# Block 0's last pair of heads placed by TensorE with 0/1 matrices instead of transfers, with one transfer per weight pair and an order of work that counts transfers

## The chip, the cores and the metric

The kernel runs on one core of one Trainium2 chip. The metric is device time in microseconds (us) of one execution; lower is better. Each kernel was run several times, in rounds that alternate with the kernel before on the same chip. An execution more than 1.5% above the fastest of its kernel counts as slow and is left out; only one in this study was (one run of the kernel before at 1269.63 us, about twice its usual time). A ratio is the mean time of one kernel's fast runs over that of the other kernel's fast runs of the same rounds, so it is not quite the ratio of the medians that are quoted beside it.

TensorE multiplies matrices, VectorE and ScalarE work on elements, GpSimd does some element work beside VectorE, and SyncE issues transfers (DMA). In the traces they are PE, DVE, ACT, POOL and SP; PEld is TensorE's loading of weights. "L466" is line 466 of the kernel's own file, so the same instruction has another number in another kernel: the up products are L466 before and L520 after.

## The reference

A linear attention with a decaying state feeds a dense layer with a gate. Cut to what matters:

```python
def _attn_ref(r, k, v, w, u):            # (4, 8, 768, 48) each; u is (8, 48)
    for t in range(S):
        cur = einsum('bhd,bhe->bhde', u[None] * kt, vt)
        y[:, :, t] = einsum('bhd,bhde->bhe', rt, state + cur)
        state = wt[:, :, :, None] * state + einsum('bhd,bhe->bhde', kt, vt)

def _moe_ref(x, w_in, w_out):            # (3072, 384), (384, 2048), (2048, 384); both weights reach the kernel as float64
    h = x @ w_in
    g = h * np.clip(h + 3.0, 0.0, 6.0) / 6.0
    return (g @ w_out).astype(np.float32)

x = attn_out.transpose(0, 2, 1, 3).reshape(B * S, H * D)     # 384 columns: 8 heads of 48
```

## The kernel before: the parts that matter here

The 768 steps of a sequence are cut into chunks of 128; there are 24 chunks in all, and three of them make a **block** of 384 rows of x. For each chunk the attention is turned into products (scans of the decay on VectorE, a score product, a masked copy, a "read"). For each block there follow 16 **ups** (x times a slice of w_in), each with a ramp on ScalarE and a gate on VectorE, and 48 **downs** (times a slice of w_out, for one chunk each). The weights arrive as float64 and are made into float32 once, pair by pair, by five passes: two on ScalarE, three on VectorE (a shift, a join and an add).

A small scheduler in the kernel (`Plan`) takes every step with an engine, an estimated duration and a priority, and emits the instructions of each engine in the order it finds. Until the first up, it fills TensorE's gaps with products of the identity ("filler"), which nobody reads; they only keep TensorE busy.

The eight heads form four pairs of 2 x 48 rows, and xT wants 3 times 128 rows: three pairs fill rows 0–47 and 64–111 of each third, and the *last pair* is cut into six pieces of 16 rows that go to the rows left free. Before the change small transfers do this, from tile x3 (named "x" in the trace) to xT:

```python
def leave(i):                                   # ScalarE: read's result out of PSUM
    ...
    for g in range(2):
        rows = slice(g * GP, g * GP + D)
        nc.scalar.copy(out=b["xT"][rows, :, now], in_=y_ps[rows, 0:3 * NCC - 2:3, :])
        nc.scalar.copy(out=b["x3"][rows, now], in_=y3[rows, :])

def last_pair(bk, c0, c1, g, q):                # three transfers of 16 rows each
    b = blocks[bk]
    cols, to = slice(c0 * L, c1 * L), g * GP + D
    for j in range(NCC):
        q.dma_start(out=b["xT"][to:to + X3, j, cols], in_=b["x3"][g * GP + j * X3:g * GP + (j + 1) * X3, cols])
...
            if c == BC - 1 or i == SPLIT - 1:   # in block 0 once for chunks 0 and 1, once for chunk 2
                c0 = 0 if i == SPLIT - 1 or bk > 0 else SPLIT
                for g in range(2):
                    q = nc.scalar if i < BC and g == 1 else nc.sync
                    plan.add(f"move{i}.{g}", "ACT" if i < BC and g else "SP", 1.8, do(last_pair, bk, c0, c + 1, g, q), ...)
```

A pair of weight slices is fetched by two transfers of 384 KB, and the priorities of the first chunks, of the weight conversions and of the ups of block 0 are constants tuned by hand:

```python
BEHIND = (-1, -1, 0, 4, 8, 10)
SPLIT = 2
START = (-52.0, -47.1, -26.0, 6.5, 11.0, 9.2)
CONV = (-45.0, 3.1)
UP = (-35.0, 1.4, -31.8, 2.0)
...
            for x in range(2):
                nc.sync.dma_start(out=to[:, x * m:(x + 1) * m], in_=srcs[x])
```

Of the kernel before, what the change touches and what calls it, by code (L numbers as in the profile page):

```python
# [8 lines left out]
F32 = mybir.dt.float32  # L9
# [9 lines left out]
L = 128  # L19
# [6 lines left out]
BEHIND = (-1, -1, 0, 4, 8, 10)  # L26
EARLY = 3
SPLIT = 2
START = (-52.0, -47.1, -26.0, 6.5, 11.0, 9.2)
CONV = (-45.0, 3.1)  # L30
UP = (-35.0, 1.4, -31.8, 2.0)
# [43 lines left out]
class Plan:  # L75
# [10 lines left out]

    def __init__(self):
        self.steps = {}
        self.rings = {}
# [4 lines left out]
    def add(self, name, engine, us, emit, after=(), key=0.0, hold=(), port=False, kb=0.0, lands=0.0):  # L94

        assert name not in self.steps, name
        self.steps[name] = (engine, us, emit, tuple(after), key, tuple(hold), port, kb, lands)

    def order(self):
        steps = self.steps  # L100
        start, end = {}, {}
        free, held = {}, {r: [] for r in self.rings}
        link = port = 0.0
        left = {n: sum(a not in end for a in x[3]) for n, x in steps.items()}
        users = {}
        for n, x in steps.items():
            for a in x[3]:
                assert a in steps, (n, a)
                users.setdefault(a, []).append(n)
        open_ = {n for n, k in left.items() if k == 0}  # L110
        out = []
        while open_:
            best = {}
            for n in open_:
                engine, us, _, after, key, hold, shared, _, _ = steps[n]
                t = free.get(engine, 0.0)
                for a in after:
                    if steps[a][0] != engine:
                        t = max(t, end[a] + self.HOP)
                for r, _ in hold:  # L120
                    over = len(held[r]) - self.rings[r]
                    if over >= 0:
                        ends = sorted(max(end[a] + (self.HOP if steps[a][0] != engine else 0.0) for a in frees)
                                      for frees in held[r] if all(a in end for a in frees))
                        if len(ends) <= over:
                            t = None
                            break
                        t = max(t, ends[over])
                if t is None:
                    continue  # L130
                if shared:
                    t = max(t, port)
                best.setdefault(engine, []).append((t, key, n))
            assert best, sorted(open_)
            t, engine = min((min(c)[0], e) for e, c in best.items())
            _, _, n = min((key, t_, n) for t_, key, n in best[engine] if t_ <= t + 1e-9)
            _, us, _, _, _, hold, shared, kb, lands = steps[n]
            start[n] = t
            free[engine] = end[n] = t + us
            if kb:  # L140

                done = max(link, end[n]) + kb / self.RATE if kb > 32 else end[n]
                link = max(link, done) if kb > 32 else link
                end[n] = max(done + self.LAND, lands)
            if shared:
                port = t + us
            for r, frees in hold:
                held[r].append(frees)
            out.append(n)
            open_.remove(n)  # L150
            for u in users.get(n, ()):
                left[u] -= 1
                if left[u] == 0:
                    open_.add(u)
        assert len(out) == len(steps), [n for n in steps if n not in end]
        self.start, self.end = start, end
        return out
# [15 lines left out]
def fast_path(tc, feat, tok, wflat, ub, moe_w_in, moe_w_out, out, flag, n_chunks):  # L173
# [18 lines left out]
    with ExitStack() as ctx:  # L192
# [20 lines left out]
        w_in = const.tile([128, NFC, NCC, 128], F32, name="w_in")  # L213
        w_out = const.tile([128, NFC, DM], F32, name="w_out")

        def constants():
# [12 lines left out]
            nc.gpsimd.tensor_copy(out=mask, in_=mask_f)  # L229

# [29 lines left out]
        def fetch(j):  # L260
            which, f = pairs[j]
            if which == "in":
                srcs = [moe_w_in[:, (f + x) * 128:(f + x + 1) * 128].rearrange("(c p) j -> p c j", p=128)
                        for x in range(2)]
                dst = w_in[:, f:f + 2].rearrange("p f c j -> p (f c) j")
            else:
                srcs = [moe_w_out[(f + x) * 128:(f + x + 1) * 128, :].rearrange("p (c j) -> p c j", j=128)
                        for x in range(2)]
                dst = w_out[:, f:f + 2].rearrange("p f (c j) -> p (f c) j", j=128)
            m = dst.shape[1] // 2  # L270
            if f64:
                bits = io.tile([128, 2 * m * 128], I64, name="bits", bufs=3)
                to = bits.rearrange("p (c j) -> p c j", j=128)
                conv[j].update(lo=bits.bitcast(U32).rearrange("p (j two) -> p j two", two=2)[:, :, 0],
                               hi=bits.bitcast(I32).rearrange("p (j two) -> p j two", two=2)[:, :, 1],
                               dst=dst.rearrange("p c j -> p (c j)").bitcast(I32))
            else:
                to = dst
            for x in range(2):
                nc.sync.dma_start(out=to[:, x * m:(x + 1) * m], in_=srcs[x])  # L280
# [22 lines left out]
        def high_low(j):  # L303
            c = conv[j]
            nc.vector.tensor_tensor(out=c["dst"], in0=c["top"], in1=c["more"].bitcast(I32), op=ALU.add)  # L305
# [102 lines left out]
        def read(i):  # L408
            d = st[i]
            first = i % n_chunks == 0  # L410
            y_ps = d["y_ps"] = pp.tile([128, 2, P, L], F32, name="two", bufs=2)
            started = set()

            def into(p, g):
                bank, at = PLACES[p]
                rows = (g ^ bank) * GP
                fresh = (bank, rows) not in started
                started.add((bank, rows))
                return dict(out=y_ps[rows:rows + D, bank, at, :], start=fresh, skip_group_check=True)

            if not first:
                for x in range(2):
                    for p in (x, 2 + x):
                        for g in range(2):
                            rows = slice(g * GP, g * GP + D)
                            nc.tensor.matmul(lhsT=d["S"][rows, p, :], rhs=d["R"][rows, p, :], stop=False, **into(p, g))  # L426
# [8 lines left out]
            for p in range(P):  # L435
                for g in range(2):
                    nc.tensor.matmul(lhsT=d["v"][:, 2 * p + g, :], rhs=d["A"][:, 2 * p + g, :],  # L437
                                     stop=(p == 1 or p == P - 1), **into(p, g))
# [22 lines left out]
        def up(bk, f, c0, c1):  # L461
# [3 lines left out]
            for j in range(NCC):  # L465
                nc.tensor.matmul(h_ps[:, :m], lhsT=w_in[:, f, j, :], rhs=b["xT"][:, j, cols],  # L466
# [95 lines left out]
        PB = NFC + BC * 4  # L562

# [5 lines left out]
        for i in range(NT):  # L569
# [37 lines left out]
            if not first:  # L607
                plan.add(f"decay{i}", "DVE" if dve else "POOL", 0.35 if dve else 0.5, do(decay, i),
                         [f"state{i - 1}", f"back{i}"], t - 0.1 if i < len(START) else t - 5, [("S", [f"read{i}"] + [f"state{i}"] * turn)], port=True)
            plan.add(f"read{i}", "PE", 1.0 + 0.55 * turn + 0.6 * (not first), do(read, i),  # L610
                     [f"above{i}"] + [f"turned{i}"] * turn + [f"decay{i}"] * (not first)
                     + [f"up{j}.{NFC - 1}" + "." * (j == 0) for j in (i // BC - 2,) if j >= 0],
                     t + 0.01, [("two", [f"leave{i}"])] + [("ps", [f"state{i}"])] * turn)
            bk, c = divmod(i, BC)
            plan.add(f"leave{i}", "ACT", 1.46, do(leave, i), [f"read{i}"], t + 0.5,
                     [("x", [f"up{bk}.{f}" for f in range(NFC)] + [f"up{bk}.{f}." for f in range(NFC)] * (bk == 0))]
                     if c == 0 else ())
            if c == BC - 1 or i == SPLIT - 1:
                c0 = 0 if i == SPLIT - 1 or bk > 0 else SPLIT
                for g in range(2):  # L620
                    q = nc.scalar if i < BC and g == 1 else nc.sync
                    plan.add(f"move{i}.{g}", "ACT" if i < BC and g else "SP", 1.8, do(last_pair, bk, c0, c + 1, g, q),
                             [f"leave{j}" for j in range(bk * BC + c0, i + 1)], k - 20, kb=1)
# [3 lines left out]
        for j in range(len(pairs)):  # L627
            t = CONV[0] + j * CONV[1]
            plan.add(f"fetch{j}", "SP", 0.9, do(fetch, j), key=t - 20, kb=768 if f64 else 384,
# [9 lines left out]
        for bk in range(NB):  # L639
            subs = [(0, SPLIT, ""), (SPLIT, BC, ".")] if bk == 0 else [(0, BC, "")]  # L640
            last_up = [f"up{bk - 1}.{NFC - 1}" + "." * (bk == 1)] if bk else []
            for c0, c1, x in subs:
                m = c1 - c0
                for f in range(NFC):
                    k = PB * bk + f if bk else UP[0] + f * UP[1] if c0 == 0 else UP[2] + f * UP[3]
                    w = f"{ready}{f // 2}"
                    name = f"{bk}.{f}{x}"
                    i = bk * BC + c1 - 1
                    plan.add(f"up{name}", "PE", 0.645 * m, do(up, bk, f, c0, c1),
                             [w] + last_up + [f"up{bk}.{f}"] * (x == ".") + [f"leave{j}" for j in range(bk * BC + c0, bk * BC + c1)]  # L650
                             + [f"move{i}.{g}" for g in range(2)], k, [("mm", [f"gate{name}"])])
# [4 lines left out]
                             [f"ramp{name}"] + [f"gate{bk}.{f}"] * (x == "."), k - 3,  # L656
                             [("g", downs)] if c0 == 0 else ())
            for c in range(BC):
                for q in range(NFC // 2):
                    k = PB * bk + NFC + c * 4 + q / 2  # L660
                    x = "." if bk == 0 and c >= SPLIT else ""
# [360 lines left out]
```

## Time and profile before

| Kernel before | |
|---|---|
| time, median of 3 runs (range) | 630.24 us (628.9 to 631.51) |
| the execution that was profiled | 626.47 us, span in the trace 624.7 us |
| TensorE busy | 604.4 us, 97% of the span |
| first up product begins | 37.27 us |
| first up product of block 1 begins | 127.01 us |

I cut the span at the two moments of the table. The view of windows of the kernel before gives for each stretch: its length, then busy time (and instructions) of PE, PEld, DVE, ACT and POOL, then TensorE's granted clock as a share of full speed, the share of the DMA engines that was busy, and GB/s.

```profile
0.00:37.27 37.27, 25.46 (x260) 23.62 (x261) 28.30 (x40) 18.47 (x39) 9.17 (x15) 0.94 0.95 279
37.27:127.01 89.74, 86.67 (x609) 63.78 (x609) 72.15 (x107) 54.06 (x137) 33.90 (x27) 0.97 0.61 189
127.01:619.30 492.29, 492.25 (x2394) 300.83 (x2394) 170.69 (x249) 143.02 (x356) 81.41 (x74) 1.00 0.26 81
```

In the last 492 us TensorE alone sets the time: it is busy throughout, at full clock. Whatever the change gains must come from the first 127 us, the **ramp**, where the clock is below 1.00 in both stretches and TensorE idles for 3.1 us of the second.

### The profile page before, as it was taken

The page shows a single profiled execution, that of the slowest core. Times are in us where ns is not written, and L with a number is a line of the kernel's source. Part 1 is how long each engine was busy: PE and PEld are TensorE (multiplying, and loading weights), DVE is VectorE, ACT ScalarE, POOL GpSimd, SP SyncE. Part 2 cuts the span into 40 slices and gives each one's busy share as a digit, 9 for nine tenths or more (in the row PEclk, how much of TensorE's full clock was granted, in tenths as well). Part 3 has the DMA queues.
Part 4 walks back from the last instruction along what each step waited for, and adds up shares of the span by engine and source line. Part 5 has one row for each costly group of instructions (what it writes and reads, how often), then busy time and mean ns, then how long its engine had stood idle before and what let it go on. Part 6 is the DMA issues. An engine that isn't in the chain of part 4 may idle for free.

```text
span 624.7 us, 8256 instructions
## 1 busy us (share of the span) xinstructions
PE 604.4 (97%) x3262; PEld 388.2 (62%) x3262; DVE 271.1 (43%) x395; ACT 216.0 (35%) x533; POOL 124.5 (20%) x115
## 2 busy tenths in 40 slices
PE   8869899999999999999999999999999999999996
PEld 7758676666565665665665665656656656555553
DVE  7939998664441652435613554215601222002200
ACT  3728773543331540334412532315403432112200
POOL 2111317641230330212312312203301000000000
PEclk9969999999999999999999999999999999999999
DMA  8956738583254621545233721301100000000000
GB/s 265 313 174 211 261 114 226 168 236 114 78 169 148 198 83 62 157 143 154 84 138 93 222 89 58 104 28 38 39 13 23 14 0 2 20 29 2 2 13 29
DMA packets 23904, 67.33 MB, mean 108 GB/s; under 512 B 2912, under 2 KB 13120, under 8 KB 23856
## 3 DMA queue, kind: packets, MB, share of 16 engines
q1 hardware_dynamic: 23392, 65.99, 33.8%
q10 hardware_dynamic: 464, 0.73, 0.4%
q8 instruction: 27, 0.44, 0.3%
q14 instruction: 21, 0.17, 0.1%
HBM read 60.81 MB, written 4.72 MB: 105 GB/s over the span
## 4 chain that ended last, share of the span: by engine, by line
PE 90%; DMA 5%; DVE 2%; ACT 1%; issue 1%; SPq 0%; ACTq 0%; DVEq 0%
PE mm L466 39%; PE mm L488 38%; PE two L371 4%; PE two L437 3%; DMA xT<-x 3%; PE two L426 2%; PE ps L433 1%; PE ps L386 1%; DMA u_bc<-in_ub_dram 1%; DMA bits<-in_moe_w_in_dram 1%; DVE A L377 0%; DVE top L300 0%; ACT more L286 0%; ACT more L290 0%; ACT r L473 0%
## 5 line engine op out<-in xcount | busy, mean ns | idle before, releaser
L466 PE MATMUL mm<-xT,w_in 128*128 128x384 f32 (+2 forms) x864 | 258.1, 456 | 10.6 <-DMA xT<-x 10.3
L488 PE MATMUL mm<-w_out,g 128*128 128x384 f32 x768 | 253.3, 488 | 0.9 <-DVE w_out L305 0.9
L466 PEld LDWEIGHTS mm<-xT,w_in 128*128 128x128 f32 x864 | 158.4, 192 | 103.2 <-issue 8.6
L488 PEld LDWEIGHTS mm<-w_out,g 128*128 128x128 f32 x768 | 144.3, 190 | 99.2 <-DVE w_out L305 1.7
L480 DVE SCALAR_TENSOR_TENSOR g<-r,mm 128x384 f32<-128x384 f32 (+2 forms) x144 | 72.8, 508 | 213.3 <-ACT r L473 212.8
L473 ACT ACTIVATE r<-mm,half 128x384 f32<-128x384 f32 (+2 forms) x144 | 78.2, 543 | 148.9 <-PE mm L466 146.5
L403 POOL TENSOR_TENSOR S<-state,E 112x192 f32<-112x192 f32 x18 | 21.6, 1202 | 241.9 <-DVE state L398 205.7
L494 ACT COPY o<-mm 128x384 f32<-128x384 f32 x24 | 11.5, 479 | 160.0 <-PE mm L488 160.0
L363 ACT ACTIVATE A<-ident,dg 128x128 f32<-128x128 f32 x192 | 60.4, 391 | 3.9 <-DVE dg L355 3.4
L451 ACT COPY xT<-two 48x384 f32<-48x384 f32 x48 | 22.7, 473 | 71.0 <-PE two L437 70.6
L325 DVE TENSOR_TENSOR_SCAN W<-feat_in,start 112x516 f32<-112x516 f32 x24 | 32.8, 1366 | 28.2 <-PE two L426 27.9
L340 POOL TENSOR_TENSOR W<-feat_in,W 112x512 f32<-112x512 f32 x21 | 26.6, 1266 | 67.0 <-DVE W L325 62.4
L377 DVE COPY_PREDICATED A<-mask,two 128x1024 f32<-128x1024 uint8 x24 | 31.5, 1311 | 16.2 <-PE two L371 13.5
L349 POOL TENSOR_TENSOR rk<-tok_in 128x384 f32<-128x384 f32 x23 | 24.3, 1056 | 60.5 <-DMA tok_in<-in_tok_dram 53.1
L316 DVE TENSOR_TENSOR_SCAN E<-feat_in,back 112x516 f32<-112x516 f32 x24 | 31.6, 1315 | 2.8 <-DMA feat_in<-in_feat_dram 2.8
L336 POOL TENSOR_TENSOR E<-feat_in,E 112x512 f32<-112x512 f32 x21 | 25.7, 1225 | 20.9 <-ACT kn L391 7.5
L371 PE MATMUL two<-W,E 48*128 48x128 f32 x384 | 27.9, 284 | 0.0
L437 PE MATMUL two<-A,tok_in 128*48 128x128 f32 x384 | 27.0, 275 | 0.6 <-DVE A L377 0.6
L350 POOL TENSOR_TENSOR rk<-rk,u_bc 128x384 f32<-128x384 f32 x23 | 26.4, 1148 | 1.8
L371 PEld LDWEIGHTS two<-W,E 48*128 48x128 f32 x384 | 23.3, 187 | 5.2 <-issue 3.3
L398 DVE TENSOR_TENSOR state<-S,ps 112x192 f32<-112x192 f32 x16 | 5.6, 352 | 46.6 <-PE ps L433 46.2
L437 PEld LDWEIGHTS two<-A,tok_in 128*48 128x48 f32 x384 | 21.1, 123 | 1.5 <-issue 0.7
(54 smaller groups left out, 273.1 us busy)
## 6 DMA issues: line engine op xcount, KB each, us to landing
feat_in<-in_feat_dram SPq DMA_DIRECT2D x23, 674.2 KB, 5.7
tok_in<-in_tok_dram SPq DMA_DIRECT2D x24, 576.0 KB, 3.9
bits<-in_moe_w_in_dram SPq DMA_DIRECT2D x16, 384.0 KB, 7.7
bits<-in_moe_w_out_dram SPq DMA_DIRECT2D x16, 384.0 KB, 3.9
bits<-in_moe_w_in_dram SPq DMA_DIRECT2D x8, 768.0 KB, 5.7
bits<-in_moe_w_out_dram SPq DMA_DIRECT2D x8, 768.0 KB, 5.4
out_dram<-o SPq DMA_DIRECT2D x24, 192.0 KB, 1.9
bits<-in_wflat_dram SPq DMA_DIRECT2D x6, 768.0 KB, 6.8
```

The source lines that it names most:

```text
L316: nc.vector.tensor_tensor_scan(out=E_[:, ::-1], data0=d["w"][:, :0:-1], data1=back.rearrange("q p t -> q (p t)")[:, ::-1], initial=0.0, op ...
L325: nc.vector.tensor_tensor_scan(out=W_, data0=d["w"][:, :-1], data1=starts[i % 2].rearrange("q p t -> q (p t)"), initial=0.0, op0=ALU.mult, ...
L340: early(i).tensor_mul(d["R"], d["r"], d["R"])
L350: eng.tensor_mul(d["rk"], d["rk"], u_bc)
L363: nc.scalar.activation(out=d["A"][:, h, :], in_=ident, func=ACT.Copy, scale=d["dg"][:, h])
L371: nc.tensor.matmul(d["a_ps"][:, g, p, :], lhsT=d["K"][rows, p, :], rhs=d["R"][rows, p, :], start=True, stop=True)
L377: nc.vector.copy_predicated(out=d["A"].rearrange("s (p g) t -> s g p t", g=2), mask=mask.rearrange("s (o x t) -> s o x t", o=1, x=1).to_br ...
L437: nc.tensor.matmul(lhsT=d["v"][:, 2 * p + g, :], rhs=d["A"][:, 2 * p + g, :], stop=(p == 1 or p == P - 1), **into(p, g))
L466: nc.tensor.matmul(h_ps[:, :m], lhsT=w_in[:, f, j, :], rhs=b["xT"][:, j, cols], start=(j == 0), stop=(j == NCC - 1))
L473: nc.scalar.activation(out=r6[:, :m], in_=b["h", f, c0][:, :m], func=ACT.Relu, bias=half, scale=1.0 / 6.0)
L480: nc.vector.scalar_tensor_tensor(out=b["g", f][:, cols], in0=b["r", f, c0][:, :m], scalar=1.0, in1=b["h", f, c0][:, :m], op0=ALU.min, op1= ...
L488: nc.tensor.matmul(b["o", c], lhsT=b["g", f][:, c * L:(c + 1) * L], rhs=w_out[:, f, :], start=(f == 0), stop=(f == NFC - 1))
```

## The change

Its intent: take the small transfers out of the way of block 0's first ups, put the weights' transfers into fewer and larger ones, let the scheduler assume that at most 8 transfers are under way at once (a constant of the kernel), and retune the order to this. Cut to its core:

```diff
-BEHIND = (-1, -1, 0, 4, 8, 10)
-SPLIT = 2
-START = (-52.0, -47.1, -26.0, 6.5, 11.0, 9.2)
-CONV = (-45.0, 3.1)
-UP = (-35.0, 1.4, -31.8, 2.0)
+BEHIND = (-1, -1, 0, 3, 6, 8)
+SPLIT = (2,)
+START = (-52.0, -52.0, -39.0, 6.5, 11.0, 7.6)
+CONV = (-45.0, 3.3)
+UP = (-38.7, 1.8, -33.2, 2.0)
 ...
+    LANES = 8
 ...
+                if kb and len(lanes) + dmas > self.LANES:
+                    t = max(t, lanes[len(lanes) + dmas - self.LANES - 1])
 ...
+            nc.gpsimd.memset(x3_0, 0.0)
+            nc.gpsimd.memset(sel, 0.0)
+            for g in range(2):
+                nc.gpsimd.tensor_copy(out=sel[:, :, g * GP + D:g * GP + D + X3],
+                                      in_=ident[0:PR, g * GP:g * GP + D].rearrange("q (j r) -> q j r", j=NCC))
 ...                                                            # fetch(j): one transfer for a pair
-            for x in range(2):
-                nc.sync.dma_start(out=to[:, x * m:(x + 1) * m], in_=srcs[x])
+                nc.sync.dma_start(out=bits.rearrange("p (a n) -> p a n", a=a), in_=src.rearrange("p a b e -> p a (b e)"))
 ...
+        def leave_last(i):                                      # ScalarE: the last pair's result, first
+            ...
+            for g in range(2):
+                rows = slice(g * GP, g * GP + D)
+                nc.scalar.copy(out=x3_0[rows, i * L:(i + 1) * L], in_=st[i]["y_ps"][rows, 1, 0, :])
+
+        def read_rest(i):                                       # TensorE: 0/1 products, then the other pairs
+            ...
+            for j in range(NCC):
+                bank, at = PLACES[j]
+                nc.tensor.matmul(d["y_ps"][:, bank, at, :], lhsT=sel[:, j, :], rhs=x3_0[:, i * L:(i + 1) * L],
+                                 start=bank not in begun, stop=False, skip_group_check=True)
 ...
+            read_state(i, (0, 2, 1))
+            write(i)
+            read_values(i, range(P - 1))
+
+        def leave_rest(i):                                      # ScalarE: one copy of all 128 rows
+            nc.scalar.copy(out=blocks[0]["xT"][:, :, i * L:(i + 1) * L],
+                           in_=st[i]["y_ps"].rearrange("q b s t -> q (b s) t")[:, 0:3 * NCC - 2:3, :])
```

Blocks 1 to 7 keep the transfers, on SyncE as before.

## The prediction

> **What bounds the kernel now.** I read the page first: TensorE is busy 604.4 of 624.7 us, the chain of waits is 90% TensorE and 5% DMA, and the slices show the clock at 6 tenths once only, in the third slice. So from about 70 us to the end TensorE is full, and only what keeps it from useful work before that can be won. The list of TensorE's waits says which:
> ```profile
> PE mm L466 <- DMA xT<-x: 10.3, 3, 8.5
> PE mm L683 <- POOL ident masks.py:199: 1.4, 1, 1.4
> PE ps L386 <- DVE E L336: 1.3, 1, 1.3
> PE mm L488 <- DVE w_out L305: 0.9, 1, 0.9
> PE two L437 <- DVE A L377: 0.6, 1, 0.6
> ```
> (us in total, times, longest.) All but a few us are waits of the first products (L466) for the small moves x to xT. TensorE's timeline shows them, after filler products (L683) have ended:
> ```profile
> 24.74 4.07 PE L683 MATMUL mm<-ident 128*128 128x128 f32 x35
> 37.27 12.07 PE L466 MATMUL mm<-xT,w_in 128*128 128x256 f32 x42 [8.46 <-DMA xT<-x]
> 49.57 6.65 PE L466 MATMUL mm<-xT,w_in 128*128 128x256 f32 x30
> 68.72 1.05 PE L466 MATMUL mm<-xT,w_in 128*128 128x128 f32 x6 [1.33 <-DMA xT<-x]
> 127.01 3.17 PE L466 MATMUL mm<-xT,w_in 128*128 128x384 f32 x9 [0.48 <-DMA xT<-x]
> ```
> 8.46 us stand before 37.27, 1.33 before chunk 2's part at 68.72, 0.48 before block 1 at 127.01 (which keeps its moves). The first 42 records cost 12.07/42 = 0.287 us, later ones about 6.49/30 = 0.216 (chain view): 3.0 us lost to a low clock. The windows show it, and that VectorE is the other full engine (columns: us, PE, PEld, DVE, ACT, POOL busy, clock, DMA share, GB/s):
> ```profile
> 20.00:30.00 10.00, 8.81 (x107) 8.13 (x105) 9.63 (x12) 7.74 (x15) 2.92 (x2) 1.00 1.05 312
> 30.00:40.00 10.00, 2.73 (x7) 2.22 (x8) 3.29 (x4) 1.75 (x2) 1.99 (x2) 0.63 0.88 254
> 40.00:50.00 10.00, 10.00 (x43) 8.57 (x42) 6.95 (x13) 5.95 (x15) 0.00 (x0) 0.86 0.18 54
> 60.00:70.00 10.00, 7.78 (x73) 5.67 (x73) 9.78 (x16) 5.23 (x11) 2.52 (x3) 1.00 0.83 257
> ```
> Why the move is late stands in the table of DMA issues and the timeline of SyncE: 16 KB take 7.2 us to land from ScalarE's queue, and SyncE's three issues last 3.92 us, from 30.71.
> ```profile
> xT<-x ACTq DMA_DIRECT2D x3, 16.0 KB, 7.2
> xT<-x SPq DMA_DIRECT2D x3, 16.0 KB, 3.7
> 30.71 3.92 SPq L458 DMA_DIRECT2D xT<-x  x3
> ```
> The x copy they need was ready at about 26.1.
>
> **The Trainium skill.** "TensorE: Matmul & The Clock Gate", The HAM clock gate, says the clock halves after an idle window of about 3.4 us and returns after a busy one as long. The trace agrees roughly: filler ends at 28.8, finer windows show 0.66 in 32 to 34, 0.50 from 34 to 42, 1.00 from 44. "DMA: Bandwidth & Descriptors", Anatomy of one DMA, gives about 2 us fixed cost whatever the size; the 24 KB moves of later blocks land in 2.0 here, so 7.2 is mostly queueing. "Trainium Kernel Development and Optimization", Key Constraints, says the queues of SP and ACT share the same 16 DMA engines: agrees, as the ACT moves were slow while the windows moved 312 GB/s. "GPSIMD Engine Reference", its specification table, says its SBUF interface is shared with VectorE: here a scan takes 1.95 us beside GpSimd's product, else 1.23.
>
> **The change part by part.**
> (1) Block 0's last pair no longer moves by DMA. For each of three chunks TensorE computes the last pair first, ScalarE copies it out (2 x 0.26 us), three products with a 0/1 matrix put it into the free rows of the same PSUM tile, and one 128-row copy (0.47, L451's size) leaves. Gone are 12 small transfers and half of the copies. Added on TensorE: 3 products of 128 columns = 6 records of 0.112 us (x12 in 1.34, chain view) = 0.67 us per chunk; chunks 0 and 1 fall into filler time, so 0.7 us lie on the path.
> (2) One transfer per weight pair (16 instead of 32 issues; rows in memory of 2 KB for w_in instead of 1 KB). It frees issue slots: SyncE's first six half-pairs took 9.31 us to issue. By itself I give it no time, since TensorE and VectorE, not DMA, hold the later ramp.
> (3) The new order. The instruction orders show K, R of chunks 0 and 1 together, chunk 2's scans before the first up product, 32 ups (2-chunk and 1-chunk parts interleaved) and only then downs, 22 in a row; score 7 moves behind the start of block 1.
>
> *First up product.* I walk VectorE's new order with durations of its groups: scan of chunk 0 at 5.5 (as now); feat 1 and tok 0 land by about 9 and 10.7 (estimates: bytes in issue order at the 226 to 335 GB/s of the first windows); two rk products 1.1, sum 0.55, K 2 x 0.68, scan 1.23 plus 0.7 for the shared port, R 2 x 0.69: 17.1. First conversion's shift and join 1.5, mask copy of chunk 0 1.3, rest 0.96, sum 0.55: 21.4. Second conversion 2.5, state 0.35, mask copy of chunk 1 1.3, decay 0.35: 25.9. Chunk 2's two scans and reciprocal 2.65, R and K 1.37, sum 0.55: 30.5. Join 1.5, state 0.35: 32.4. The sum at 30.5 lets ScalarE make four diagonals (1.3) and then, in its order, the copy of chunk 1 (0.47): 32.2. The state at 32.4 frees the PSUM tile for the four turns (0.5). So the first up is at about **33.2** instead of 37.27, with no TensorE gap over 3 us before it, so at full clock.
>
> *TensorE from there to block 1.* Now 127.01 - 37.27 = 89.7. Less waits 0.88 + 1.33 + 0.48 + small ones of 0.5 = 3.2, slow clock 3.0, score 2, turn 2 and score 7 which leave this stretch (1.09 + 0.5 + 1.09 = 2.7), plus 0.7: 81.5. Unhindered, block 1 starts at 114.7. The old start that compares is 127.01 - 1.09 = 125.9. Gain **11.2**.
>
> *VectorE's limit.* Up to the last w_out conversion (ends at 89.8) it is busy 73.2 us (windows to 90), 1.6 of them before 5.5. The new order has the same work before that point (one sum less). So it cannot end before 5.5 + 71.6 = 77.1, and with 4 to 5 us of waits (landings, gates waiting for TensorE) at about 81.5. The first chunk's last two downs need it, and what follows is fixed: 2 downs 1.3, 32 downs 20.6 (0.645 each), four scores 4.4, two turns 1.0, reads of chunks 3 to 6 7.6: 34.9, so block 1 starts at 116.4. Gain 9.5, and 0.4 off for its own move, which waits as now. That is the later of the two limits and I take it: about **9 us**. From block 1 on both kernels do the same, and the 5.4 us between the last product and the end stay.
>
> 630.2 - 9.0 = 621.2.
>
> **Rivals.** (A) VectorE or ScalarE takes the wait's place fully. For: VectorE is 92 to 98% busy in most windows from 50 to 100, and in the new order its in-order gates wait for TensorE. Each us of VectorE idle beyond my 4 to 5 costs one. At 10 us of idle the gain is 4: 626. (B) The move was all that mattered, and the limit of VectorE does not bite: 11 to 13 us, as the first up may start at 30 if the shared port and landings cost less: 617 to 619. Against: the sum of 77.1 without any idle. (C) The new transfer order delays data: bigger transfers land as a whole, so a conversion waits for all 768 KB, feat 2 for a slot. If weights 2 to 7 come 4 us late, TensorE stalls among the ups and its clock falls again: 625 to 629. Against: at 330 GB/s the bytes before pair 2 (6.4 MB) are in by about 23.5, and it is wanted at 30. (D) Order in later blocks makes a new wait for moves, as one block's six moves are issued with a store between: 0 to 3 us slower. For: the wait of 0.48 shows little slack.
>
> **Range and chances.** A is the main risk upward, B downward: 616.5 to 626. Over 2% faster means under 617.6, which needs B almost whole: 0.13. Slower by 2% would need two new stalls of 10 us: 0.01. The rest, 0.86, is within 2%.
>
> **What would show it.** Right: no wait of L466's successor for xT before block 1, clock 1.00 in every window to 100, first up at 33 (31 to 35), last w_out conversion ending at 80 to 83, first 384-column up at 115 to 118, a wait for w_out among the first 16 downs of 1 to 4 us, 6 records x 3 for the 0/1 products. Wrong if: the first up comes after 36, or the waits of TensorE for VectorE's w_in or w_out exceed 5 us, or block 1 onward takes more than now (492.3 us from the first 384-column product to the last one's end at 619.3, plus 1.1 for score 7).

## The result

| | Kernel before | Changed kernel |
|---|---|---|
| median of 4 runs (range), same rounds | 629.57 us (628.22 to 631.51) | 618.97 us (618.55 to 619.33) |
| profiled execution: time, span | 626.47, 624.7 | 618.55, 616.7 |
| first up product | 37.27 | 33.75 |
| last w_out conversion ends | 89.8 | 82.22 |
| first up of block 1 | 127.01 | 117.64 |

The ratio of fast runs is 0.983, with a 95% interval of 0.980 to 0.986: 1.7% faster, inside the 2% that count as the same. The time lies 2.2 us below the predicted 621.2 and inside the range. The traces differ by 8.0 us in span, the medians by 10.6: the profiled run of before was 3.1 us faster than its median, that of the changed kernel 0.4. So about 2.6 us of the gain in the medians is a thing that these two traces do not contain. The record says where to look for it, because it lists TensorE's mean granted clock for each timed run. In the four later batches the kernel before has 43 fast runs; the 12 with a clock of 0.984 took 629.9 to 632.1 us, the 13 with 0.990 or more took 624.5 to 629.8, and the profiled run had 0.991. A mean of 0.984 is about 20 us at half clock, one of 0.991 about 11 (an estimate: twice the missing share of the span). The changed kernel's first four runs had 0.996 to 0.999. So the extra gain goes with a longer stretch of low clock that most runs of the kernel before have and its profiled run has not; no trace of such a run was kept, so this is likely and not shown.

The same cut of the changed kernel's span, in the view of windows (columns as before), and two of its windows of 10 us that answer to those in the prediction:

```profile
0.00:33.75 33.75, 27.22 (x274) 24.68 (x275) 28.61 (x40) 18.64 (x44) 10.22 (x19) 1.00 0.84 275
33.75:117.64 83.89, 81.71 (x580) 60.01 (x578) 71.49 (x108) 50.93 (x122) 33.11 (x27) 1.00 0.67 211
117.64:612.00 494.36, 493.49 (x2411) 301.72 (x2410) 170.62 (x249) 145.99 (x367) 83.15 (x75) 1.00 0.25 81
...
30.00:40.00 10.00, 9.34 (x84) 7.57 (x82) 9.93 (x16) 7.06 (x17) 2.85 (x2) 1.00 0.34 100
...
60.00:70.00 10.00, 9.68 (x62) 8.72 (x60) 8.72 (x19) 9.71 (x22) 0.60 (x1) 1.00 0.67 220
```

The clock is 1.00 in every stretch. In the second, TensorE is idle for 2.2 us instead of 3.1 and busy for 81.7 instead of 86.7: the slow clock, a score, a turn and score 7 are gone from it. From block 1 on the work is 493.5 us, which is the 492.3 of before plus the 1.1 of score 7 that moved there. Between 30 and 40 us, where TensorE stood still before (2.73 of 10), both TensorE and VectorE are now nearly full (9.34 and 9.93).

TensorE's waits of the changed kernel (us in total, times, longest):

```profile
PE ps L399 <- DVE E L349: 2.5, 1, 2.5
PE mm L520 <- DVE g L534: 1.5, 4, 0.7
...
PE mm L542 <- DVE w_out L317: 0.5, 1, 0.5
```

The 10.3 us for xT are gone; none took their place in full. The first line is before the first up, in filler time. After it, TensorE waits four times for a gate and once for a w_out conversion. TensorE's timeline shows these (start, duration, group, and in brackets the idle time before it and what ended that):

```profile
21.19 0.83 PE L482 MATMUL two<-x,sel 112*128 112x128 f32 x6
...
33.75 4.06 PE L520 MATMUL mm<-xT,w_in 128*128 128x256 f32 x18
...
56.41 4.20 PE L520 MATMUL mm<-xT,w_in 128*128 128x128 f32 x24 [0.73 <-DVE g L534]
...
82.28 5.43 PE L542 MATMUL mm<-w_out,g 128*128 128x384 f32 x16 [0.50 <-DVE w_out L317]
...
117.64 8.01 PE L520 MATMUL mm<-xT,w_in 128*128 128x384 f32 x24
```

The first 18 records of the ups take 4.06 us, 0.226 each, against 0.287 before. The 0/1 products (L482) are six records per chunk, as counted in the prediction.

What set the first up is best read from the chain of waits of the same kernel before 33.75 (start, duration, engine, tile and line; each piece was released by the one before it or followed it on its engine):

```profile
19.68 0.94 DVE w_in L317
20.63 0.46 DVE dg L368
...
26.17 0.24 DVE S L416
...
30.37 0.46 DVE dg L368
30.83 0.48 DVE top L307
31.33 1.66 DVE top L312
32.99 0.28 DVE state L411
```

From 10.3, where the first values land, to 33.3 the chain is VectorE, with two pieces of 1.7 us together that it names "issue". Not a transfer is among them. The prediction walked VectorE's order step by step to the same points: sum after the first conversion 21.4 (here 20.63 + 0.46 = 21.1), decay of chunk 1 done at 25.9 (26.4), sum of chunk 2 at 30.5 (30.8), state at 32.4 (33.3), first up at 33.2 (33.75).

### The profile page after: what moved, and what is told of

It is laid out like the page before. It is cut to its first block, busy times and chain, and to the rows that moved or that the text cites. A ratio compares the mean times of both kernels' runs of the same rounds, so it can differ in the third digit from the quotient of the medians.

```text
span 616.7 us, 8184 instructions
## 1 busy us (share of the span) xinstructions
PE 602.4 (98%) x3262; PEld 386.4 (63%) x3262; DVE 270.7 (44%) x395; ACT 215.6 (35%) x530; POOL 126.5 (21%) x119
## 4 chain that ended last, share of the span: by engine, by line
PE 89%; DVE 7%; DMA 1%; ACT 1%; issue 1%; SPq 0%; DVEq 0%; ACTq 0%
PE mm L542 39%; PE mm L520 38%; PE two L384 4%; PE two L452 3%; PE two L435 2%; PE ps L445 2%; PE ps L399 2%; DVE top L312 1%; DMA tok_in<-in_tok_dram 1%; DVE top L307 1%; DVE w_in L317 1%; DVE w_out L317 1%; DVE E L349 1%; DVE g L534 1%; DVE E L329 0%
## 5 line engine op out<-in xcount | busy, mean ns | idle before, releaser
L520 PE MATMUL mm<-xT,w_in 128*128 128x384 f32 (+2 forms) x864 | 254.7, 453 | 1.7 <-DVE g L534 1.5
L520 PEld LDWEIGHTS mm<-xT,w_in 128*128 128x128 f32 x864 | 155.6, 190 | 91.8 <-DVE g L534 3.3
L505 ACT COPY xT<-two 48x384 f32<-48x384 f32 x42 | 19.8, 472 | 72.9 <-PE two L452 72.5
L338 DVE TENSOR_TENSOR_SCAN W<-feat_in,start 112x516 f32<-112x516 f32 x24 | 31.5, 1314 | 28.1 <-PE two L435 28.0
L349 POOL TENSOR_TENSOR E<-feat_in,E 112x512 f32<-112x512 f32 x21 | 27.6, 1313 | 21.1 <-issue 8.6
L363 POOL TENSOR_TENSOR rk<-rk,u_bc 128x384 f32<-128x384 f32 x23 | 24.8, 1080 | 1.8
L452 PEld LDWEIGHTS two<-A,tok_in 128*48 128x48 f32 x384 | 21.1, 123 | 1.7 <-issue 0.9
```

Source lines behind the costliest of these rows:

```text
L338: nc.vector.tensor_tensor_scan(out=W_, data0=d["w"][:, :-1], data1=starts[i % 2].rearrange("q p t -> q (p t)"), initial=0.0, op0=ALU.mult, ...
L349: early(i).tensor_mul(d["K"], d["k"], d["K"])
L452: nc.tensor.matmul(lhsT=d["v"][:, 2 * p + g, :], rhs=d["A"][:, 2 * p + g, :], stop=True, **into(i, p, g))
L520: nc.tensor.matmul(h_ps[:, :m], lhsT=w_in[:, f // 2, j, f % 2, :], rhs=b["xT"][:, j, cols], start=(j == 0), stop=(j == NCC - 1))
```

## The experiments

**The theory** before the runs: the gain is the wait for xT together with the lowered clock behind it, cut short by VectorE's total of work up to the last w_out conversion. **The rivals**: the move alone matters and VectorE does not bind; or the new order and the larger transfers do the work and the 0/1 products add little; or the clock alone was the loss. All runs below gave correct results, except one. The kernel before was run again in each batch of rounds, with medians of 628.44, 628.65, 629.14 and 629.8 and single runs from 624.5 to 633.4; a batch's runs share one chip.

### 1. Only the clock: filler before the first ups (kernel before)

```diff
                 last = self.start[n] + us
+                if n == self.until:
+                    for _ in range(34):
+                        self.spin()
                 spinning = n != self.until
```

> The kernel before with 34 more filler products in the gap before the first up product, nothing else. Theory (the clock term of the prediction): the first up still starts at about 37.3 us, held by the moves, but the clock stays at 1.00, so the first 42 records cost 0.216 instead of 0.287 us: 2.5 to 3.5 us faster than before (ratio about 0.995). Rival (only the wait itself costs, the clock would come back alone or its loss is hidden behind VectorE): under 1 us.

Measured: 625.63 (624.65 to 627.57) against 628.44; ratio 0.9959 (0.9934 to 0.9985). The timed gain is 0.9 to 4.1 us. TensorE's timeline of this kernel:

```profile
37.26 9.30 PE L469 MATMUL mm<-xT,w_in 128*128 128x256 f32 x42 [1.04 <-DMA xT<-x]
...
67.50 1.41 PE L469 MATMUL mm<-xT,w_in 128*128 128x128 f32 x6 [3.28 <-DMA xT<-x]
68.70 2.77 PE L491 MATMUL mm<-w_out,g 128*128 128x384 f32 x4
```

The filler does what it should: the same 42 records take 9.30 us instead of 12.07, so 2.8 us are won. But TensorE then comes earlier to chunk 2's part, and that has its own small transfers: the wait there is 3.28 instead of 1.33, and behind it the clock is low again (four down records take 2.77 us; after the change 16 take 5.43). Block 1 starts at 127.04, as before (127.01). So in this pair of traces the whole of the clock's 2.8 us was given back at the next transfer.

The timed runs say otherwise: their median gain is 2.8 us, inside the 2.5 to 3.5 of the theory and clear of the rival's 1. The two readings need not clash. The pair of traces sets a fast run of the kernel before (626.47, clock 0.991) beside a run of this one that is slower than its median (626.52). In the timed runs the median clock is 0.988 before and 0.996 with the filler. So the filler's gain is there in the medians and was nothing in the traced pair: filling the first gap does not secure it, because the next transfer can lower the clock again.

### 2. Only the placement: 0/1 products with the old constants and two transfers per pair

```diff
-BEHIND = (-1, -1, 0, 3, 6, 8)   START = (-52.0, -52.0, -39.0, 6.5, 11.0, 7.6)   CONV = (-45.0, 3.3)   UP = (-38.7, 1.8, -33.2, 2.0)
+BEHIND = (-1, -1, 0, 4, 8, 10)  START = (-52.0, -47.1, -26.0, 6.5, 11.0, 9.2)   CONV = (-45.0, 3.1)   UP = (-35.0, 1.4, -31.8, 2.0)
-    LANES = 8
+    LANES = 10 ** 6
 ...                                            # fetch(j): two transfers again, and 0.9 instead of 0.45 us for their issue
+                for x in range(2):
+                    ...
```

> Part 1 alone: the last pair placed by TensorE, with the old order constants, two transfers per weight pair and an order that does not count transfers. Theory: most of the gain comes from this part, 619 to 623, no wait of TensorE for xT before block 1. Rival (placement needs the new order and the single transfers to pay, as VectorE takes the wait's place): 624 to 628, with TensorE waits for VectorE's w_in or w_out of 5 us or more.

Measured: 617.62 (617.47 to 618.58) against 628.44; ratio 0.9835 (0.981 to 0.986), which cannot be told from the changed kernel's 0.9829. **The placement alone has the whole gain.** In its trace the first up starts at 28.72, 5.0 us earlier than in the changed kernel, and yet block 1 starts at 117.96, with score 7 (1.1 us) done before it: 116.9 on the changed kernel's count, 0.8 earlier. The windows from its first up to its last up, and on to block 1, show where five us went:

```profile
28.72:72.10 43.38, 38.80 (x266) 33.27 (x267) 41.71 (x77) 36.75 (x82) 10.24 (x8) 1.00 0.82 269
72.10:117.96 45.86, 45.86 (x350) 29.46 (x348) 33.37 (x39) 18.95 (x56) 28.92 (x21) 1.00 0.50 147
```

Among the ups VectorE is busy 41.71 of 43.38 us, and TensorE is idle for 4.6: 2.5 in waits for gates, 1.2 for chunk 2's scan, 0.7 for ScalarE's copy of the last pair. In the changed kernel the ups end at 72.6, here at 72.1; there TensorE idles 1.7 us between them. So of the 5.0 us of earlier start 2.9 go into more idle time and 1.6 into work that the changed kernel does before its first up (chunk 2's score above all); 0.5 are left at the end of the ups. After 72.1 TensorE is full; the changed kernel has its wait of 0.5 us for w_out there. This is the shortage of VectorE that the prediction counted, met at the gates and the scan, and not at the last w_out conversion, which ends at 79.2 here and holds nobody.

### 3. The new order without the placement

```diff
-            if bk == 0:
+            if False:
                 plan.add(f"first{i}", "PE", ...
 ...
-                if c == BC - 1:
+                if c == BC - 1 or i == SPLIT[0] - 1:
+                    c0 = 0 if i == SPLIT[0] - 1 or bk > 0 else SPLIT[0]
                     for g in range(2):
+                        q = nc.scalar if i < BC and g == 1 else nc.sync
```

> The changed kernel with block 0's last pair moved by transfers again (two small groups per part, from SyncE and ScalarE), all else as changed: order constants, one transfer per pair, counting of transfers. Theory (the moves are the cost): TensorE waits for xT again before the first up, 5 us or more, and the time is 625 to 629, 6 to 10 us slower than the changed kernel. Rival (the new order of work made the gain): within 2 us of the changed kernel, 618 to 621.

Measured: 622.01 (620.47 to 623.31) against 628.44; ratio 0.99 (0.9875 to 0.9924). It keeps 6.4 of about 10.7 us; I had given the transfers' return more. The first up starts at 33.84, as in the changed kernel: the new order makes chunks 0 and 1 together and so early that the last of their transfers lands at 33.79 by the trace, while filler still runs. It releases the first up; that this is the moment at which VectorE's state releases it in the changed kernel is a coincidence. TensorE's waits for xT are down to 0.5 us in all. What is lost shows first in ScalarE's timeline, with its queue of transfers (ACTq) in it, and then in TensorE's:

```profile
43.28 2.05 ACTq L512 DMA_DIRECT2D xT<-x  x3
45.38 1.21 ACT L527 ACTIVATE r<-mm,half 128x256 f32<-128x256 f32 x3 [2.13 <-PE ps L399]
```

```profile
46.89 1.56 PE L520 MATMUL mm<-xT,w_in 128*128 128x256 f32 x6 [2.48 <-DVE g L534]
```

For 2.05 us ScalarE does nothing but issue three transfers. Three ramps stand behind them, their gates on VectorE behind those, and TensorE waits 2.48 us at 46.89. But the landing stands right behind. The chain of waits of this kernel passes ScalarE's three earlier issues (30.23 to 32.10, for chunks 0 and 1); at chunk 2 it passes a transfer that SyncE issued at 43.48, which the next group of ups wants:

```profile
43.48 5.36 DMA xT<-x
...
48.98 1.73 PE mm L520 x12
```

So in this kernel the small transfers stand in the way twice, by the time that their *issue* takes from an engine in the chain and by their landing 5.36 us after it. Had ScalarE been free of the issue, TensorE would presumably have come to chunk 2's ups earlier and waited there. How much either is worth alone is not shown: no run takes the issue away, for instance by giving all these transfers to SyncE. The placement removes both. Part of what it removes the new order removes too (the wait before the first up), which would be why order alone (6.4) and placement alone (10.8) do not add up to the change.

### 4. The changed kernel with the old constants

```diff
-BEHIND, START, CONV, UP of the changed kernel
+BEHIND, START, CONV, UP of the kernel before
```

> The changed kernel with the old order constants (START, CONV, UP, BEHIND), so placement, single transfers and counting. Theory: the constants are worth 0 to 3 us (619 to 622). It differs from place_only by single transfers and counting alone; theory: within 1 us of it. Rival: the constants are worth 4 us or more (623 and up).

Measured: 617.75 (617.49 to 618.35) against 628.44; ratio 0.9837 (0.9812 to 0.9862). It differs from run 2 only in the single transfers and the counting of transfers, and is within 0.2 us of it: these two parts are worth nothing that can be measured. With the placement in, the new constants add nothing either; first up at 28.53, block 1 at 118.26 with score 7 and a turn before it.

### 5. Two transfers per pair in the changed kernel

```diff
-                nc.sync.dma_start(out=bits..., in_=src...)
+                for x in range(2):
+                    nc.sync.dma_start(...)                  # half of it
-            plan.add(f"fetch{j}", "SP", 0.45, ...)
+            plan.add(f"fetch{j}", "SP", 0.45, ..., dmas=2)
```

> The changed kernel with each weight pair fetched in two transfers again, counted as two by the order. Theory (transfers are hidden in the ramp): within 1 us of the changed kernel, 618 to 620. Rival (the slots that the single transfers free are what lets the new order start early): 621 or more.

Measured: 620.26 (619.42 to 621.33) against 629.14; ratio 0.9861 (0.9826 to 0.9897). The changed kernel, repeated in other rounds (run 8), has the same ratio. Together with run 4 this is all there is on the larger transfers: within 0.2 us in the old order (same rounds), and level in the new one, where the rounds differ and the intervals leave about 2 us open.

### 6. More work for VectorE: the join of the eight w_out pairs done twice

```diff
             nc.vector.scalar_tensor_tensor(out=c["top"], in0=c["hi"], scalar=-0x40000000, in1=c["top"], ...)
+            if j >= 8:
+                nc.vector.scalar_tensor_tensor(out=c["top"], in0=c["hi"], scalar=-0x40000000, in1=c["top"], ...)
```

> The changed kernel with one VectorE instruction done twice (the join, 0.96 us, of the eight w_out pairs; the result stays right): 7.7 us more work on VectorE before the last w_out conversion. Theory (VectorE now sets the ramp, and the last conversion has no slack): that conversion ends at about 90 instead of 82, and the time is 6 to 8 us longer than the changed kernel. Rival (TensorE alone sets it, VectorE has slack): under 2 us.

The second join changes nothing in the result. Measured: 626.99 (625.24 to 628.69), 7.5 us more than the changed kernel in the same rounds (619.44), for 8 x 0.96 = 7.7 us of added work. TensorE's waits:

```profile
PE mm L523 <- DVE g L537: 5.0, 5, 1.3
PE mm L545 <- DVE w_out L320: 3.8, 2, 2.0
```

They grow from 2.0 to 8.8 us. This shows that work added to VectorE before the last w_out conversion (which now ends at 90.1, 7.9 later) delays block 1's start (125.67, 8.0 later) one for one.

### 7. Less work for VectorE: no join for the eight w_in pairs (wrong result)

```diff
+            if j >= 8:
-            nc.vector.scalar_tensor_tensor(out=c["top"], in0=c["hi"], scalar=-0x40000000, in1=c["top"], ...)
+                nc.vector.scalar_tensor_tensor(out=c["top"], in0=c["hi"], scalar=-0x40000000, in1=c["top"], ...)
```

> The changed kernel with the join left out for the eight w_in pairs (signs are lost, so the result is wrong on purpose): 7.7 us less work on VectorE, 3 of them before the first up. Theory: first up at about 31, TensorE's 2 to 3 us of waits for VectorE inside the ramp vanish, 4 to 6 us faster than the changed kernel. Rival (landings of weights or ScalarE take over at once): under 1.5 us.

The weights of w_in lose their sign and top exponent bit here, so the result is wrong (relative error 1.44); the times of the instructions show no sign of it (a down record 486 ns in both kernels, a gate 555 and 554, in the median). Measured: 616.64 (615.77 to 617.2), 2.8 us less than the changed kernel for 7.7 us less work: between theory and rival. The first up comes only 1.2 us earlier than in the first trace of the changed kernel, at 32.59 (1.7 earlier than in run 8's, which has the same low clock before it as this one); from there to block 1 at 115.16 TensorE takes 82.6 us with 1.1 us of waits. That is TensorE's own work (81.7 busy in the changed kernel). So in the changed kernel the two engines are nearly level from the first up on: add work to VectorE and all of it shows, take work away and TensorE soon holds.

### 8. The changed kernel again

> The changed kernel, unchanged, on the chip and in the rounds of the three runs beside it. 618 to 620, ratio to before 0.980 to 0.986, as in its first measurement; needed to compare the others with it and with place_only, which came out level.

Measured: 619.44 (618.44 to 622.74) against 628.65; ratio 0.9861 (0.9824 to 0.9898). It repeats the result, with a wider spread than the first four runs had (618.55 to 619.33). In this profile the gap in the filler before the first turn (the transposes of chunk 0, L399) was 3.6 us instead of 2.5, and the window shows a clock of one half behind it, which the first profile had not:

```profile
16.00:18.00 2.00, 2.00 (x14) 1.72 (x14) 2.00 (x4) 0.77 (x3) 0.00 (x0) 0.50 1.00 242
```

Everything after it lies 0.6 to 0.9 us later (first up at 34.31, block 1 at 118.50). The length of the gap alone does not tell when this happens. In run 6 the gap at this place was shorter than the first profile's, and the clock fell all the same:

```profile
13.61 1.01 PE L402 MATMUL ps<-ident,E 112*128 112x112 f32 x4 [2.33 <-DVE E L352]
```

The window from 14 to 16 us of that trace has a clock of 0.50. In run 5 the gap was 3.11 us and the clock stayed at 1.00. So the changed order has one gap after which the clock falls in some executions. That this makes the spread of the timed runs is not shown: the fastest two of the six (618.44 and 618.49) do have the highest clocks, 0.999 and 1.000, and the slowest (622.74) the lowest, 0.992, but the next slowest (621.42) has 0.997.

### 9. Four attempts at a better order

The experiments above say that VectorE is short of time during the ups. So three kernels have the placement, the single transfers, the old constants, and the w_out conversions at 10, 20 or 30 lower priority, with block 0's downs taken pair by pair over the three chunks so that they can use each w_out pair as it comes. A fourth only starts chunk 2 a little earlier with the old constants. (The lines cut from the edit also make block 0's downs wait for its last ups, and block 1's ups for block 0's downs.)

```diff
-            t = CONV[0] + j * CONV[1]
+            t = CONV[0] + j * CONV[1] + (10.0 if j >= NFC // 2 else 0.0)      # 20.0, 30.0
 ...
-                    k = PB * bk + NFC + c * 4 + q / 2
+                    k = PB * bk + NFC + (c * 4 + q / 2 if bk else q * 1.5 + c / 2)
```

> A try at a better version: placement and single transfers with the old constants, w_out conversions of lower priority, and block 0's downs taken pair by pair over all three chunks, so that a w_out pair is wanted every 3.9 us instead of every 1.3. Theory (conversions compete on VectorE with what the ups need): TensorE is left with no waits for w_out and few for gates, 612 to 616. Rival (VectorE's total is the limit whatever the order): 617 to 620.

> As q_old10, with the w_out conversions of still lower priority: five of eight come after the last gate of the ups instead of three. Theory (in q_old10 conversions that nobody wants yet still stand ahead of gates on VectorE, and the ups wait for gates): waits of the ups for gates shrink from 2.0 to about 1 us, 614.5 to 616.5. Rival (the ups are held by the chain of three PSUM tiles, ScalarE and VectorE, whatever the priority): 617 to 618.

> The same with seven of the eight conversions after the last gate. Theory: the waits for gates are gone, but the downs may now wait for w_out, as a pair is wanted every 3.9 us and VectorE also scans chunks 3 to 5: 613 to 618, best if no wait for w_out appears. Rival: 617 or more.

The fourth:

```diff
-START = (-52.0, -47.1, -26.0, 6.5, 11.0, 9.2)
+START = (-52.0, -47.1, -31.0, 6.5, 11.0, 9.2)
```

> A last try at a better version: the changed kernel with the old constants but chunk 2's start set between the old and the new one (-31; old -26, new -39). Theory: in the old constants TensorE waits 3 us for chunk 2 (scan, mask copy, ScalarE's copy), in the new ones the first up is 5 us later; between them both shrink, 615 to 617. Rival (VectorE's total work sets the end of the ramp, so only the place of the wait changes): 617 to 619.

| Run | median (range) | ratio (95%) | first up | TensorE's waits for gates / w_out | block 1 |
|---|---|---|---|---|---|
| +10 | 617.41 (617.19 to 617.55) | 0.9819 (0.9784 to 0.9854) | 28.61 | 2.3 / 0 | 117.98 |
| +20 | 620.23 (618.95 to 623.48) | 0.9863 (0.9823 to 0.9902) | 28.53 | 4.6 / 0 | 118.28 |
| +30 | 620.45 (619.6 to 621.62) | 0.9869 (0.9834 to 0.9905) | 28.41 | 1.4 / 2.7 | 120.15 |
| chunk 2 earlier | 618.13 (617.75 to 619.07) | 0.9827 (0.9791 to 0.9863) | 28.50 | 4.0 / 0.9 | 117.04 |

(Block 1's start may have scores, turns or reads of later chunks before it or leave them behind it, so it compares only roughly.) All four are misses as attempts: none is clearly below the 617.6 of run 2. The waits move between the gates and w_out, and the time does not fall with them; of the orders tried none helps. Two of them also lose the clock: behind the waits of 2.24 us (+20) and 2.68 us (+30) the windows show 0.50 in 70 to 72 and in 84 to 86. The one with +10 was timed in the same rounds as run 8, and its five runs all lie below all six of the changed kernel, by 2.0 us in the medians. So it beats the changed kernel, by 0.3%. Runs 2 and 4, with the same constants, are at 617.6 and 617.8 in other rounds, so the old constants are the likely reason, and not the later conversions.

## Why the prediction was right

- **The bound.** It named the waits for xT, 10.3 us in all, as nearly all that could be won, with the low clock behind them. After the change there is no wait for xT before block 1. Run 2 shows that the placement alone makes the gain.
- **The first up.** 33.2 predicted, 33.75 measured, with every station of the walk through VectorE's order within 0.9 us. The walk worked because it followed the engine that is full.
- **The clock.** 1.00 in all windows to 100 us, as said; the 3.0 us are gone from this stretch. Two things are weaker than they look. "At full clock" before the first up holds in this trace, and not in the repeat, where the clock was 0.50 in 16 to 18 (run 8). And the sum treats the clock as a term that stands by itself; run 1 gained 2.8 us with it in the medians, but in the trace all of it was lost again at the next small transfer.
- **TensorE's own time.** 81.5 predicted from first up to block 1, 81.7 busy measured; the 0/1 products cost 0.67 us for the six records that lie on the path, as worked out.
- **VectorE's limit.** Last w_out conversion at 81.5 predicted, 82.2 measured; VectorE has 72.4 us of work after 5.5 instead of 71.6 and idles for 4.3, where 4 to 5 were allowed. Run 6 confirms the mechanism at its full size, 7.5 us for 7.7.
- **The split of the waits was mis-sized.** "A wait for w_out among the first 16 downs of 1 to 4 us" was 0.5. In its place stand 1.5 us of waits for gates, earlier, among the ups. Both are VectorE's lateness; the step that failed is the thought that TensorE would run unhindered through the ups and meet the limit in one place.
- **Block 1's start and the size.** 116.4 predicted, 117.64 measured, so the traced gain of 8.0 us is 1.0 below the predicted 9.0. The timed gain is 10.6, 1.6 above it. The difference between the two is not the changed kernel but the spread of the kernel before, whose profiled run was a fast one; the prediction subtracted a gain read from that run from a median 3.8 us above it. So the gain was overestimated by 1.0 and the baseline's own loss left out, and the two errors partly cancel: that 621.2 lies only 2.2 us off is in part luck. The kernel before varies with its clock (see the result); which of its waits lowers the clock in the slower runs is not settled.
- **Rival A** (another engine takes the wait's place) holds in part: TensorE now waits 2.0 us for VectorE, which idles for 4.3, within the 4 to 5 that the prediction allowed. **Rival B** said that a first up at 30 would bring 11 to 13 us. Run 2 has its first up at 28.7 and gains no more: the step from an early first up to an early end fails as soon as another engine sets the end. By the time alone B could not be dismissed, as 618.97 lies in its 617 to 619; what decides against it is that VectorE does bind (run 6). **Rival C** (larger transfers come late) did not show, and the larger transfers did not help either (runs 4 and 5). **Rival D** (later blocks slower) did not show: 493.5 us, against 492.3 + 1.1.
- **Part 3, the order,** was counted as what brings the first up forward. With the old order it comes even earlier, at 28.4 to 28.7, once the transfers are gone. The walk was right for the kernel at hand, and silent on which part deserved the credit; only undoing the parts one by one told.

## What to carry to other kernels

When a small transfer stands on the critical path, look for the engine that can put the data in place itself, and count the transfer's issue time on the engine that issues it as well as its landing. Before counting a removed wait as gain, add up the work of the next fullest engine up to the point where its result is needed: here that sum, plus 4 to 5 us of idle time, gave the new end within 1 us, and an earlier start brought nothing past it. When a change has several parts, put each back alone: here one part had all of the gain, and the retuned order, worth 6.4 us by itself, added nothing to it.

## What the Trainium skill lacked or had wrong

- "DMA: Bandwidth & Descriptors", Issuing engines are not separate DMA queues, says that the time to initiate a transfer is usually small beside the transfer. For small ones it is less so: three transfers held ScalarE for 2.05 us in run 3, where each took 2.3 to 5.0 us from issue to landing, and for 1.88 and 2.21 us in the kernel before. The page does not say what this does to a compute engine that issues them; here a wait of TensorE of 2.48 us stood behind it.
- "DMA: Bandwidth & Descriptors", Anatomy of one DMA, has a fixed cost of about 2 us, fitted on GpSimd's path. On SyncE's queue the 24 KB moves of later blocks land in 1.9 to 2.0 us, which agrees; among weight loads the moves on ScalarE's queue in the kernel before took 4.3 to 7.4, and the page has no figure for a small transfer in a queue behind large ones.
- "TensorE: Matmul & The Clock Gate", The HAM clock gate, gives one idle window of about 3.4 us. Here the length of a gap does not tell by itself: the clock halved at gaps of 2.33 us (run 6), 2.68 (run 9, +30), 3.28 (run 1), 3.31 (run 7) and 3.6 (run 8), and stayed at 1.00 at 2.45 (the first profile), 2.75 (run 3) and 3.11 (run 5). In runs 1 and 8 it fell after the gap, with TensorE at work again (from about 68 in run 1, work having resumed at 67.5). The page says that the window runs freely, which may be why; no run here moves a gap and nothing else. In the kernel before, full clock came back 5 to 7 us after work resumed at 37.27, later than the one busy window of 3.4 us of the page's table; a window that runs freely leaves room for up to two.
- "GPSIMD Engine Reference", the specification table, says that VectorE shares an interface with GpSimd, but not what that costs; the prediction put in 0.7 us by eye. Only that page lacks it: "SBUF — State Buffer", Who interferes with whom, has the rule that the later one is blocked until the other's instruction ends. The trace agrees: the join, which has two inputs in SBUF and starts at 31.33, takes 1.66 us beside a GpSimd product that the profile ends at about 32.2 (such spans are rough), against 0.96 for the joins with no GpSimd product beside them.
